# Thirteen sections of a fused Fourier and attention kernel: the same slots of the two row halves in another order

## The chip, the cores and the metric

The kernel runs on one core of a Trainium2 chip. The metric is the device time of one execution in microseconds (us): 1698.75 us, the median of 1699.33, 1698.75 and 1698.6.

## The reference, cut to what matters

The input is one sequence of 2048 tokens with 512 features. Two branches are mixed by a gate per token.

```python
g = _sigmoid((x * gate_w).sum(-1, keepdims=True))
a = _A_ref(x, ...)   # y = dft_seq_re @ (x @ dft_hid_re.T) - dft_seq_im @ (x @ dft_hid_im.T)
b = _B_ref(x, B_wqkv, B_wo)
return g * a + (1 - g) * b
...
H = 32; Dh = D // H                                  # 32 heads of 16 features
scores = jnp.einsum("bhqd,bhkd->bhqk", q, k) * scale
p = _softmax(scores, axis=-1)
o = jnp.einsum("bhqk,bhkd->bhqd", p, v)
return (lambda x, *d: x.transpose(*d))(o, 0, 2, 1, 3).reshape(B, S, D) @ wo
```

The last line's `@ wo` is the projection whose matmuls are the nine products of this document.

## The kernel before, in words

The kernel takes the heads in 16 pairs; one head of a pair lives in rows 0 to 63 of the matmul array, the other in rows 64 to 127. A matmul that contracts over only 64 rows occupies one half of the array, and two of them, one in each half, run side by side. All work of the main part is written as such pairs, in an order written out by hand; no scheduler changes it. Each engine executes its own list of instructions in that order.

There are four kinds of matmul in this part, each into one PSUM bank of 128x512.

- `a` (line 284, `a_tile`): keys by queries transposed the other way, to find the row maximum of the scores. VectorE reads the bank with a maximum reduction (line 286).
- `s` (line 774, `scores`): the scores with the maximum already subtracted through two extra rows. ScalarE reads the bank with the exponential into `pt` (line 775).
- the product (line 451, `Chain.mm`, tile `d`): in the sections that matter here a 64-row half of one of the nine products of a token tile's projection. Three head groups with three products each (high and low parts of the operands) make nine; each is done once in each half of the rows, so that eighteen matmuls add up in one bank of its own (`psD`, one buffer). After the eighteenth, `finish` (line 646) lets ScalarE scale the bank into `few`, and GpSimd adds it to the output tile (line 647).
- the values step (line 796, `pv`), written `|`: four heads' worth of `pt` times the values into one accumulating bank `acc`. Each fp32 matmul of it is recorded twice, so a step shows as eight.

`a` and `s` have three banks each, `psA` and `psS`. A new tile of a kind takes the bank of that kind that was used longest ago, so the fourth `a` waits until VectorE has read the first, and the fourth `s` until ScalarE has read the first.

A pattern is a text of slots, walked by `segment` (line 907) once for each row half; its first text is half 0, the second half 1. A slot of one letter is a pair: first a product in the current half, then a score (`s` or `a`) in the other half. A slot of two letters is a double: two scores and no product, the first letter in the other half and the capital in the current half. `|` is a values step. In half 1, the first product of a section waits for the reader of the scores that stood after the last product of half 0 (line 940), because the two halves of a sum may not be written into the bank at once. The product is issued before the score of its slot, and `finish` is issued right behind the eighteenth product, ahead of that slot's score.

Patterns follow each other: `START`, 13 times `THIN`, 96 times `FULL` (the Fourier sums over the sequence), 13 times `NINE`, and then a tail written out in `whole` (line 992). `NINE` takes nine products per section, eight sections from the projection of the second half of the tokens and five from the first. When the last maximum of a pair of heads and half of the tokens is issued, two follow-ups are put into `deferred`: `m_parts` (line 293: a small reduction on VectorE and two small operations on GpSimd) and `m_rows` (line 301: a transpose on VectorE and eight small DMAs that write the two extra rows of `qs`, on SP's queue and on GpSimd's). In a `NINE` section one of them is run behind the first `|` of a half that has a second one (line 925), or at the end of a half (line 949).

Of the kernel before, what the change touches and what calls it, by code (L numbers as in the profile page):

```python
# [31 lines left out]
def mix_kernel(ctx: ExitStack, tc: tile.TileContext, xa_t, xa, wqkv, w_hid, w_seq, wo, gate_w, out):  # L32
# [776 lines left out]
    def take(gen, n, whole=True):  # L809

        got = []
        while len(got) < n:
            x = next(gen, None)
            if x is None:
                break
            x[0].left -= 1
            got.append((*x, x[0].left == 0))
            if whole and got[-1][4]:
                break
        return got  # L820
# [56 lines left out]
    FULL = "s2 a3 s4 a1 s5 s2 a0 s3 a4 s1 a5 s2 a0 s3 a4 a1 | |"  # L877
    START = "sA s aS - - a s - - a s - - a", "s a s a s a s a s a s a +s +a"
    THIN = "s a s a s a s a s a | s a aS sA |", "aS a s s a s a s a s | s a a sA |"
    NINE = "a s a s a s a s a | sS sA aA |", "aS s a s a s s a aS | s a sA sA |"  # L880

    def stream(h):

# [23 lines left out]
    def segment(pattern, half, ds, stop):  # L907
# [5 lines left out]
        for n, slot in enumerate(pattern.split()):  # L913
# [3 lines left out]
            if slot == "|":  # L917
# [5 lines left out]
                while between:  # L923
                    between.pop(0)()
                if deferred and pattern in NINE and not turned and "|" in pattern.split()[n + 1:]:
                    deferred.pop(0)()
# [21 lines left out]

        if deferred and not (pattern in NINE and (turned or len(deferred) == 1)):
            deferred.pop(0)()  # L950

    def pairs():
# [5 lines left out]
        for gen, n in ((proj(1, (0, 1, 2), one), 8), (first, 5)):  # L958
            for i in range(n):
                yield NINE, take(gen, 9)  # L960

# [86 lines left out]
```

## Time and profile before

| what | value |
|---|---|
| runs | 1699.33, 1698.75, 1698.6 us |
| span of the profiled execution | 1696.8 us (its own device time is not listed; the runs lie 1.8 to 2.5 us above this span) |
| TensorE busy | 1689.2 us, 100% of the span |
| VectorE busy | 1366.7 us, 81% |
| ScalarE busy | 1138.6 us, 67% |
| GpSimd busy | 449.6 us, 26% |
| the 13 sections | 1489.68 to 1632.47 us of the span |
| the tail behind them | 1632.47 to 1696.80 us |

Times are counted from the start of the span. A matmul of 64 rows is recorded with 0.39 us, but two halves and two successive matmuls overlap, so busy time says little about TensorE: the distance between the starts of successive matmuls is what counts. A row of a timeline gives the start, the duration, the engine, the line, the operation, the tiles and, in brackets, the idle time of the engine before it with what ended that. PE is the matmul, PEld the load of its weights, DVE is VectorE, ACT is ScalarE, POOL is GpSimd, SP the queue that issues most DMAs.

### The profile page before, as it was taken

How to read it: one execution, taken by the hardware profiler on the slowest of the kernel's cores; microseconds unless marked ns; L12 is line 12 of the kernel's file. 1: busy time of each engine (PE TensorE's matmuls, PEld its weight loads, DVE VectorE, ACT ScalarE, POOL GpSimd, SP SyncE). 2: the span in 40 equal slices, each digit the busy share in tenths (PEclk: the TensorE clock that was granted, in tenths of full speed). 3: DMA queues.
4: the chain of work that ended last, by engine and by line, in shares of the span. 5: the costliest groups of instructions: out<-in, count | busy, mean ns of one | idle time of the engine just before them, and what ended most of it. 6: DMA issues, size and time to landing. Idle time of an engine off the chain costs nothing.

```text
span 1696.8 us, 33721 instructions
## 1 busy us (share of the span) xinstructions
PE 1689.2 (100%) x13040; PEld 1076.1 (63%) x13040; DVE 1366.7 (81%) x2313; ACT 1138.6 (67%) x2242; POOL 449.6 (26%) x554
## 2 busy tenths in 40 slices
PE   9999999999999999999999999999999999999998
PEld 7888855556666666666666666666666666655544
DVE  5439888888888888888888888888888888889854
ACT  5212377777766777666777677776667776678886
POOL 0101122322222333222222343322323343211110
PEclk9999999999999999999999999999999999999999
DMA  8963600314141434314156435224141535362114
GB/s 294 344 146 132 161 8 13 47 39 76 57 76 46 88 98 97 73 39 82 38 95 243 96 108 109 68 63 77 50 83 58 120 111 101 129 187 39 36 30 138
DMA packets 82274, 165.10 MB, mean 97 GB/s; under 512 B 19460, under 2 KB 19954, under 8 KB 78274
## 3 DMA queue, kind: packets, MB, share of 16 engines
q1 hardware_dynamic: 77874, 161.99, 37.1%
q8 instruction: 103, 1.69, 0.4%
q0 software_dynamic: 3808, 0.30, 0.2%
q10 hardware_dynamic: 432, 0.66, 0.1%
q14 instruction: 57, 0.47, 0.1%
HBM read 107.73 MB, written 54.52 MB: 96 GB/s over the span
## 4 chain that ended last, share of the span: by engine, by line
PE 99%; DMA 0%; DVE 0%; DVEq 0%; ACT 0%; SPq 0%; issue 0%
PE d L451 33%; PE acc L796 27%; PE s L774 14%; PE a L284 12%; PE s L365 3%; PE s L397 1%; PE d L365 1%; PE acc L782 1%; PE a L106 1%; PE s L107 1%; PE a L107 1%; PE s L106 1%; PE s L105 1%; PE a L105 1%; PE s L451 1%; PE a L451 0%
## 5 line engine op out<-in xcount | busy, mean ns | idle before, releaser
L286 DVE TENSOR_REDUCE mx<-a 128x1 f32<-128x512 f32 x2026 | 1239.9, 681 | 213.1 <-PE a L284 199.1
L775 ACT ACTIVATE pt<-s 128x512 f32<-128x512 f32 x2006 | 1023.2, 620 | 403.0 <-PE s L774 390.5
L774 PE MATMUL s<-qs,ks 50*128 50x512 f32 x2006 | 794.0, 422 | 0.0
L284 PE MATMUL a<-ks,qs 48*128 48x512 f32 x2026 | 744.5, 398 | 0.0
L451 PE MATMUL d<-xab,ch 64*128 64x512 f32 x2016 | 647.8, 396 | 0.0
L774 PEld LDWEIGHTS s<-qs,ks 50*128 50x128 f32 x2006 | 365.4, 185 | 228.5 <-issue 177.5
L796 PE MATMUL acc<-pt,vt 128*17 128x512 f32 x3968 | 484.2, 596 | 0.0
L284 PEld LDWEIGHTS a<-ks,qs 48*128 48x128 f32 x2026 | 370.3, 186 | 53.2 <-DVE mx L286 23.2
L451 PE MATMUL d<-xab,cl 64*128 64x512 f32 x1008 | 399.4, 396 | 0.0
L451 PEld LDWEIGHTS d<-xab,ch 64*128 64x128 f32 x2016 | 366.7, 184 | 21.6
L435 POOL CAST ch<-craw 128x512 fp32r<-128x512 f32 x126 | 77.1, 612 | 549.1 <-PE a L284 282.2
L796 PEld LDWEIGHTS acc<-pt,vt 128*17 128x17 f32 x3968 | 102.3, 96 | 184.7 <-issue 184.5
L451 PEld LDWEIGHTS d<-xab,cl 64*128 64x128 f32 x1008 | 185.7, 184 | 10.5
L436 POOL TENSOR_TENSOR cl<-craw,ch 128x512 fp32r<-128x512 f32 x126 | 162.1, 1287 | 10.2
L309 POOL DMA_DIRECT2D qs<-mt x119 | 67.0, 568 | 150.3 <-DVE mt L303 147.8
L451 PE MATMUL d<-wre,xab 64*128 64x512 f32 x336 | 90.5, 402 | 0.0
L451 PEld LDWEIGHTS d<-wre,xab 64*128 64x128 f32 x336 | 59.0, 185 | 38.4 <-issue 23.3
L451 PE MATMUL d<-wo_hl,o_hl 64*128 64x512 f32 (+1 forms) x246 | 68.1, 409 | 0.0
L451 PEld LDWEIGHTS d<-wo_hl,o_hl 64*128 64x128 f32 (+1 forms) x246 | 42.3, 185 | 29.5 <-issue 12.1
L101 ACT CAST hl<-s 128x512 fp32r<-128x512 f32 x28 | 16.1, 587 | 58.5 <-PE s L365 31.4
L647 POOL TENSOR_TENSOR yp<-yp,few 128x512 f32<-128x512 f32 x12 | 15.4, 1283 | 112.4 <-ACT few L646 112.4
L469 POOL CAST xab<-y 128x512 fp32r<-128x512 f32 x16 | 9.8, 611 | 127.8 <-ACT y L467 99.6
(168 smaller groups left out, 1009.6 us busy)
## 6 DMA issues: line engine op xcount, KB each, us to landing
craw<-w_seq SPq DMA_DIRECT2D x128, 256.0 KB
qk<-hl SPq DMA_DIRECT2D x32, 512.0 KB
qs<-qk SPq DMA_DIRECT2D x96, 128.0 KB
ks<-qk SPq DMA_DIRECT2D x96, 128.0 KB
b<-hl SPq DMA_DIRECT2D x16, 512.0 KB
xab<-b SPq DMA_DIRECT2D x16, 512.0 KB
o<-oe SPq DMA_DIRECT2D x62, 128.0 KB
oh<-nh SPq DMA_DIRECT2D x12, 512.0 KB
```

The costliest lines, as they stand in the source:

```text
L105: nc.tensor.matmul(ps, sh, mh, start=first, stop=False)
L106: nc.tensor.matmul(ps, sh, ml, start=False, stop=False)
L284: nc.tensor.matmul(ps, qs[p % 2][r, qt * P:(qt + 1) * P], ks[p % 2][r, kb * 512:(kb + 1) * 512], start=True, stop=True)
L286: user = nc.vector.tensor_reduce(mx[p % 2][:, h, qt, kb:kb + 1], ps, AX.X, ALU.max)
L309: (nc.gpsimd if own else nc.sync).dma_start(rows.rearrange("v (q b c) -> v b q c", q=8, b=4)[:, b], mt[hf][32 * b + h:32 * b + 32:2])
L365: i = nc.tensor.matmul(ps, st[r], mv[r], start=not half and not j, stop=half == 1 and j == 11)
L435: nc.gpsimd.tensor_copy(h1, raw)
L436: nc.gpsimd.tensor_tensor(l1, raw, h1.bitcast(F32), ALU.subtract)
L451: i = nc.tensor.matmul(self.ps, st[r], mv[r], start=not self.begun, stop=stop)
L774: nc.tensor.matmul(ps, ks[p % 2][rr, kt * P:(kt + 1) * P], qs[p % 2][rr, q0:q0 + 512], start=True, stop=True)
L775: return nc.scalar.activation(pts[u][:, 2 * qb + h], ps, AF.Exp, bias=0.0, scale=DH ** -0.5)
L796: i = nc.tensor.matmul(acc[32 * j:32 * j + 17], vt[:, kt, p, 16 * h:16 * h + 17], pt[:, j], start=kt == 0, stop=kt == NT - 1)
```

## The change

Only the text of the pattern `NINE` changes. A section keeps 18 single slots and 7 doubles, 16 `s`, 16 `a` and four values steps, and each stream of scores keeps its count in each section. What changes is the order, and so where the doubles stand and how many `a` stand near each other.

```diff
     FULL = "s2 a3 s4 a1 s5 s2 a0 s3 a4 s1 a5 s2 a0 s3 a4 a1 | |"
     START = "sA s aS - - a s - - a s - - a", "s a s a s a s a s a s a +s +a"
     THIN = "s a s a s a s a s a | s a aS sA |", "aS a s s a s a s a s | s a a sA |"
-    NINE = "a s a s a s a s a | sS sA aA |", "aS s a s a s s a aS | s a sA sA |"
+    NINE = "s a s a s s a aS | aS a s sA |", "aS aA sS | sA a s s a a a s a s |"
```

Before, half 0 is nine singles, a values step, three doubles and a values step; half 1 is a double, seven singles and a double, a values step, two singles and two doubles, and a values step. After, half 0 is seven singles and a double, a values step, a double, two singles and a double, and a values step; half 1 is three doubles, a values step, a double and nine singles, and a values step. The lists of GpSimd and SP are the same in both kernels; those of TensorE, ScalarE and VectorE differ only in the order within the sections, and at the last section's end.

## The prediction

> **What bounds the kernel now.** I read the page first, for the engine that carries the span.
>
> ```profile
> span 1696.8 us, 33721 instructions
> PE 1689.2 (100%) x13040; PEld 1076.1 (63%) x13040; DVE 1366.7 (81%) x2313; ACT 1138.6 (67%) x2242; POOL 449.6 (26%) x554
> PE 99%; DMA 0%; DVE 0%; DVEq 0%; ACT 0%; SPq 0%; issue 0%
> ```
>
> TensorE makes 99% of the chain that ended last. So what counts is where its list stands still. Next the view by windows, for four sections (busy time and count per engine, then the granted clock), and the row of `few`, the reader of each section's sum:
>
> ```profile
> 1500.63:1511.71 11.08, 11.08 (x86) 5.54 (x82) 10.07 (x19) 8.82 (x19) 3.86 (x8) 1.00 0.21 78
> 1511.71:1522.74 11.03, 11.03 (x87) 5.59 (x83) 9.91 (x17) 9.23 (x20) 1.30 (x2) 1.00 0.42 71
> 1533.66:1544.58 10.92, 10.92 (x88) 5.55 (x84) 9.84 (x17) 8.84 (x19) 1.28 (x2) 1.00 0.18 61
> 1621.55:1632.47 10.92, 10.92 (x82) 5.26 (x79) 7.84 (x13) 8.83 (x19) 3.07 (x4) 1.00 0.24 69
> L646 ACT ACTIVATE few<-d,omg x13: 681/682/682, 1499.6 to 1631.4; 128x512 f32<-128x512 f32 x13
> ```
>
> Twelve distances in 131.8 us: a section takes 10.98 us. VectorE is busy for 9.8 to 10.1 of that (third group), so it has one microsecond to spare, on average over the section only.
>
> The timeline of one section gives the prices of TensorE:
>
> ```profile
> 1534.00 0.39 PE L774 MATMUL s<-qs,ks 50*128 50x512 f32 x1
> 1535.40 0.40 PE L774 MATMUL s<-qs,ks 50*128 50x512 f32 x1
> 1535.64 0.42 PE L284 MATMUL a<-ks,qs 48*128 48x512 f32 x1
> 1536.97 0.72 PE L774 MATMUL s<-qs,ks 50*128 50x512 f32 x3
> 1538.85 0.50 PE L284 MATMUL a<-ks,qs 48*128 48x512 f32 x1
> 1539.20 0.50 PE L774 MATMUL s<-qs,ks 50*128 50x512 f32 x1
> 1540.23 0.40 PE L774 MATMUL s<-qs,ks 50*128 50x512 f32 x1
> 1540.56 0.50 PE L774 MATMUL s<-qs,ks 50*128 50x512 f32 x1
> 1540.90 0.39 PE L284 MATMUL a<-ks,qs 48*128 48x512 f32 x1
> 1542.46 0.50 PE L774 MATMUL s<-qs,ks 50*128 50x512 f32 x1
> 1543.26 0.39 PE L284 MATMUL a<-ks,qs 48*128 48x512 f32 x1
> 1544.58 0.50 PE L284 MATMUL a<-ks,qs 48*128 48x512 f32 x1
> ```
>
> Pair to pair: six in 1.40 us (1534.00 to 1535.40), 0.235 each. Across a values step: 1535.64 to 1536.97 and 1543.26 to 1544.58, 1.32. The pair behind a step needs 0.34 to the next, since its weights are not loaded ahead: it is recorded with 0.50 in place of 0.39, so it truly runs 0.11 later than recorded. Any pair that waits pays the same 0.11 again (1540.56 with 0.50, next at 1540.90).
>
> **The change part by part.** A section has 25 pairs in four stretches, before and after. Without waits it takes 4 x (0.34 + 1.32) + (25 - 8) x 0.235 = 10.64 us in either order. So the old order holds 0.34 us of waits, and the question is what the new order holds.
>
> The waits are for banks. Their clocks are the readers':
>
> ```profile
> 1537.77 4.87 DVE L286 TENSOR_REDUCE mx<-a 128x1 f32<-128x512 f32 x8 [0.47 <-PE a L284]
> 1501.36 0.68 DVE L286 TENSOR_REDUCE mx<-a 128x1 f32<-128x512 f32 x1
> 1501.96 0.68 DVE L286 TENSOR_REDUCE mx<-a 128x1 f32<-128x512 f32 x1
> 1502.10 0.18 PEld L284 LDWEIGHTS a<-ks,qs 48*128 48x128 f32 x1
> 1502.69 0.18 PEld L284 LDWEIGHTS a<-ks,qs 48*128 48x128 f32 x1 [0.16 <-DVE mx L286]
> 1489.68 0.50 PE L284 MATMUL a<-ks,qs 48*128 48x512 f32 x1
> 1490.25 3.08 DVE L286 TENSOR_REDUCE mx<-a 128x1 f32<-128x512 f32 x5 [0.82 <-PE a L284]
> 1490.03 0.39 PE L774 MATMUL s<-qs,ks 50*128 50x512 f32 x1
> 1490.45 2.06 ACT L775 ACTIVATE pt<-s 128x512 f32<-128x512 f32 x4 [1.54 <-PE s L774]
> ```
>
> A reduction lasts 0.68 and the next starts (4.87 - 0.68) / 7 = 0.60 later. The fourth and fifth `a` load their weights 0.05 to 0.06 after the ends, 2.04 and 2.64, of the reductions three before them. So an `a` is recorded no earlier than the start of the third reduction before it plus 0.73, and truly runs 0.11 later. The first `a` behind a values step meets its reduction after 0.57; a later one after 0.46. An `s` meets its exponential after 0.42; exponentials follow every (2.06 - 0.60) / 3 = 0.49.
>
> *Removed.* The four-`s` run in old half 1 (wait 1540.23 to 1540.56, and its 0.11: 0.2 together) and the wait of the first product in half 1 (1538.85 to 1539.20 is behind a step, and 1539.20 again carries 0.50: 0.11). That is 0.31 of the 0.34. In the new order that product stands behind eight more scores, so its condition is long met.
>
> *Added, the run of `a`.* Number the new section's slots 1 to 25. After the third values step come 16 `sA`, 17 `a`, 18 `s`, 19 `s`, 20 `a`, 21 `a`, 22 `a`, 23 `s`, 24 `a`, 25 `s`. Count from slot 16. Without waits: slots 17 to 25 at 0.34, 0.58, 0.81, 1.05, 1.28, 1.52, 1.75, 1.99, 2.22, next section at 3.54. Reductions: of 16 at 0.57, of 17 at 1.17, of 20 at 1.77. Slot 21 needs the bank of 16: 0.57 + 0.73 = 1.30, truly 1.41, 0.13 late. Slot 22 needs that of 17: 1.90, truly 2.01 in place of 1.64: another 0.37. Then 23 at 2.25, 24 due at 2.48 needs 20's: 2.50, truly 2.61: 0.13. So 25 stands at 2.85, the next section at 4.17: **+0.63**.
>
> *Added, three doubles in a row.* From slot 9 (first behind a step): reductions of 9, 10 and 12 at 0.57, 1.17, 1.77. Slot 13 comes at 0.81 + 1.32 = 2.13, slot 14 at 2.47; its second `a` needs the bank of 12: 2.50, truly 2.61: **+0.14**. The `s` waits of half 0 (slots 6 and 8) come to 0.02 each, **+0.04**.
>
> Sum: 10.64 + 0.63 + 0.14 + 0.04 = 11.45 us a section, against 10.98: **+0.46**. The same arithmetic on the old order gives 10.96 to 11.06, so I trust it to about 0.05.
>
> *Moved, the end of the sum.* The eighteenth product now stands in the last slot, and the next section's first product needs its bank back from `few`. Before, two singles' rest and two doubles lay between.
>
> ```profile
> 1499.07 0.60 ACT L775 ACTIVATE pt<-s 128x512 f32<-128x512 f32 x1 [0.56 <-PE s L774]
> 1499.56 0.68 ACT L646 ACTIVATE few<-d,omg 128x512 f32<-128x512 f32 x1
> 1542.46 0.18 PEld L451 LDWEIGHTS d<-wo_hl,o_hl 64*128 64x128 f32 x1 [0.85 <-issue]
> 1544.57 0.18 PEld L451 LDWEIGHTS d<-wo_hl,o_hl 64*128 64x128 f32 x1 [0.85 <-ACT few L646]
> ```
>
> The 0.85 before 1544.57 is put down to `few`, but 1542.46 has the same 0.85 with no `few`: it is the values step. In the new order, product 25 truly runs at 2.85; taking the 0.42 of an exponential, `few` starts at 3.28, ends at 3.96, frees the bank at 4.01; the product is due at 4.17. Hidden by the values step, with 0.16 to spare. If `few` were half a microsecond later, about 0.35 would show; both ends are kept.
>
> *Moved, the follow-ups and their DMAs.* The lists of GpSimd and SP do not change. The transpose comes behind four reductions of half 0 in place of five.
>
> ```profile
> 1504.58 2.73 SPq L309 DMA_DIRECT2D qs<-mt  x4
> 1504.85 2.24 POOL L309 DMA_DIRECT2D qs<-mt  x4 [2.81 <-DVE mt L303]
> 1515.03 0.50 PE L774 MATMUL s<-qs,ks 50*128 50x512 f32 x2
> qs<-mt POOLq DMA_DIRECT2D x119, 2.0 KB, 1.7
> ```
>
> The rows are written from 1504.58 on and first used at 1515.03, a section later; the issues end by 1507.3, a landing takes 1.7. New first use: slot 8, 1.75 us into its section, where it was at 3.3 (1511.71 to 1515.03). Some 5 us of cover remain; price nothing.
>
> *Last section.* One half's `a` stream runs out: the section in the row 1621.55 has 12 reductions. In the new order slots 20 to 24 lose their `a`, so its run costs nothing: 10.82 against 10.92, -0.1. The tail keeps its list; its start meets one exponential less in ScalarE's queue and an earlier last maximum; 0, within 0.3.
>
> Total: 12 x 0.46 - 0.1 = **+5.4 us**. The span goes from 1696.8 to 1702.2; the median of the runs lies 1.95 above the span, which I keep: 1704.1 us.
>
> *A rule against the change.* All quoted windows show the clock at 1.00, with waits in them. The Trainium skill, "TensorE: Matmul & The Clock Gate", section "A second HAM failure mode: psum-queue depth-cycling", says that cycling through PSUM banks can let TensorE idle briefly so often that its clock drops back to half. No run here shows it. If it held, a pair would cost 0.47: 25 x 0.235 x 13 = 76 us more, by estimate some 1780 us.
>
> **The rivals.** *The waits are dearer:* `few` shows as well, 0.35 more in each of twelve sections: 5.4 + 4.2 = +9.6, 1708.4 us. Against it stand the 0.16 to spare.
>
> *The waits are half as dear:* a waiting `a` does not pay the 0.11, because the product ahead of it in its slot is already running. Then the run costs 0.37, the doubles nothing: 10.64 + 0.41 = 11.05 to 11.18, at most +0.2 a section, +2.3: 1701.0 us. For it: slot 22's product is issued before its wait. Against it: 1540.56, where exactly that happened.
>
> *Faster:* the banks of the `a` run come free in time, in slots 21 to 24. Then only the removed waits count: 10.82 or less against 10.98, -0.16 x 13 = -2 to, without any wait, -4.4: 1694.3 us. It decides when the new waits, 0.81 by my sum, stay under 0.34 a section. With reductions 0.45 apart in place of 0.60 the run alone would still hold 0.35, and the row of eight shows 0.60.
>
> *The clock rule* above is the last.
>
> **How the numbers follow.** Forecast, +0.3 to +0.6 a section, 0.68; dearer 0.10; half as dear 0.14; faster 0.07; clock 0.01. The likeliest gives 1704.1. The range runs from the half-price end, 1701.0, to just under the dear end, 1708.0. A measurement tells about 0.2%, 3.4 us: the first two and the clock are slower, 0.79; half price falls within, 0.14; faster 0.07.
>
> **What would show it.** The distance of `few` rises to 11.4; weight loads of `a` wait on the reduction in slots 21, 22 and 24, with 0.3 to 0.4 in slot 22; the waits of line 451 on the exponential in half 1 vanish; the 0.85 before a section's first product stays 0.85 (a higher number is the dear rival); the clock stays 1.00. I am wrong if reductions start sooner after their `a` than 0.46, or if waits are hidden behind the products.

## The result and the profile after

The changed kernel takes 1703.36 us, the median of 8 runs (1702.99 to 1703.73), against 1698.66 us for the kernel before on the same chip: a ratio of 1.0027, with a 95% interval of 1.0017 to 1.0038. The forecast was 1704.1 us, slower, with a range of 1701.0 to 1708.0.

The page of the changed kernel, its span and its busy times per engine:

```profile
span 1701.5 us, 33708 instructions
PE 1693.1 (100%) x13040; PEld 1068.7 (63%) x13040; DVE 1368.5 (80%) x2313; ACT 1140.5 (67%) x2242; POOL 449.6 (26%) x554
```

The span is 4.7 us longer. The counts of instructions per engine are those of before, and the busy times of VectorE and ScalarE are 1.8 and 1.9 us higher: hardly anything was added but waiting. The view by windows puts it in its place. First the kernel before, then the changed one; each has the thirteen sections in the first row and the tail in the second (busy time and count per engine, the granted clock, the DMAs):

```profile
1489.68:1632.47 142.79, 142.79 (x1066) 71.85 (x1063) 126.74 (x211) 115.40 (x224) 25.98 (x35) 1.00 0.28 75
1632.47:1696.80 64.33, 58.17 (x381) 27.37 (x377) 24.88 (x44) 46.57 (x95) 7.40 (x6) 0.99 0.30 97
```

```profile
1489.87:1637.17 147.30, 146.88 (x1067) 69.03 (x1063) 128.08 (x212) 117.55 (x224) 25.73 (x35) 1.00 0.27 72
1637.17:1701.50 64.33, 58.15 (x381) 27.32 (x377) 24.50 (x42) 46.39 (x94) 7.66 (x6) 0.97 0.32 98
```

The sections grow by 4.51 us, the tail is the same to the hundredth, and 0.19 lies ahead of the first section. The clock stays at 1.00 in the sections; in the tail it is 0.97 in place of 0.99, with the same length.

The timeline of one section of the changed kernel: its first product, the first pair behind each values step, then the waiting `a` of the last stretch, the section's eighteenth product beside the last of them, and the next section's first product:

```profile
1535.35 0.49 PE L451 MATMUL d<-wo_hl,o_hl 64*128 64x512 f32 x1
1538.43 0.49 PE L284 MATMUL a<-ks,qs 48*128 48x512 f32 x1
1540.56 0.50 PE L284 MATMUL a<-ks,qs 48*128 48x512 f32 x1
1542.54 0.50 PE L774 MATMUL s<-qs,ks 50*128 50x512 f32 x1
1543.85 0.50 PE L284 MATMUL a<-ks,qs 48*128 48x512 f32 x1
1544.45 0.50 PE L284 MATMUL a<-ks,qs 48*128 48x512 f32 x1
1545.05 0.49 PE L284 MATMUL a<-ks,qs 48*128 48x512 f32 x1
1545.05 0.49 PE L451 MATMUL d<-wo_hl,o_hl 64*128 64x512 f32 x1
1546.69 0.50 PE L451 MATMUL d<-wo_hl,o_hl 64*128 64x512 f32 x1
```

The section takes 11.34 us. Its stretches take 3.08, 2.13, 1.98 and 4.15; the prediction's terms for them add up to 3.11, 2.13, 2.04 and 4.17. Counted from slot 16 (1542.54), slots 21, 22 and 24 stand at 1.31, 1.91 and 2.51; the prediction had 1.30, 1.90 and 2.50. The three stand 0.60 apart, which is the distance of VectorE's reductions and none of the 0.235, 0.34 and 1.32 of TensorE's pairs.

The weight loads of that stretch say the same, and the end of a section shows `few`:

```profile
1544.45 0.18 PEld L284 LDWEIGHTS a<-ks,qs 48*128 48x128 f32 x1 [0.41 <-DVE mx L286]
1545.05 0.18 PEld L284 LDWEIGHTS a<-ks,qs 48*128 48x128 f32 x1 [0.30 <-DVE mx L286]
1546.69 0.18 PEld L451 LDWEIGHTS d<-wo_hl,o_hl 64*128 64x128 f32 x1 [0.85 <-ACT few L646]
...
1545.72 0.68 ACT L646 ACTIVATE few<-d,omg 128x512 f32<-128x512 f32 x1
```

`few` ends at 1546.40, 0.29 before the first product of the next section, whose 0.85 is the usual idle time behind a values step.

Last, the waits of TensorE's weight loads over all sections (engine, tile and line, what it waited for: us in total, times, longest). Before:

```profile
PEld a L284 <- DVE mx L286: 11.5, 16, 0.9
PEld d L451 <- ACT pt L775: 1.2, 8, 0.2
PEld s L774 <- ACT pt L775: 1.2, 5, 0.3
```

and after:

```profile
PEld a L284 <- DVE mx L286: 30.9, 51, 0.9
PEld s L774 <- ACT pt L775: 11.0, 13, 0.9
```

These lists also hold the 0.85 of idle time behind a values step, put down to whatever came last. Of the 16 waits of `a` before, 13 are such 0.85, and of the 51 after, 26. Without them the waits of `a` for VectorE rise from 3 of 0.16 us to 25 of 0.24 to 0.41: from 0.5 to 8.8 us. The 13 waits of `s` after are 0.85 too, so the 5 of before, up to 0.3, are gone, and those of a product for an exponential, which the prediction expected to go, are in the list no more.

### The profile page after: what moved, and what is told of

Read it like the earlier page. It is cut to its first block, busy times and chain, and to the rows that moved or that the text cites. A ratio compares the mean times of both kernels' runs of the same rounds, so it can differ in the third digit from the quotient of the medians.

```text
span 1701.5 us, 33708 instructions
## 1 busy us (share of the span) xinstructions
PE 1693.1 (100%) x13040; PEld 1068.7 (63%) x13040; DVE 1368.5 (80%) x2313; ACT 1140.5 (67%) x2242; POOL 449.6 (26%) x554
## 4 chain that ended last, share of the span: by engine, by line
PE 99%; DMA 0%; DVE 0%; issue 0%; DVEq 0%; ACT 0%; SPq 0%
PE d L451 33%; PE acc L796 27%; PE s L774 14%; PE a L284 13%; PE s L365 3%; PE s L397 1%; PE d L365 1%; PE acc L782 1%; PE s L106 1%; PE s L105 1%; PE a L106 1%; PE a L105 1%; PE a L107 1%; PE s L107 1%; PE s L451 1%; PE a L451 0%
```

## The experiments

The theory: a bank comes free at the pace of its reader, 0.60 us for VectorE's reduction, and an `a` that comes before the third reduction ahead of it has ended waits for that. The rivals are named in each expectation. All experiments compare with the same kernel before, at 1698.6 to 1698.75 us. The section's length is taken from the first and the last of the thirteen `few`, divided by twelve.

### The five `a` of the last stretch set apart

```diff
-    NINE = "s a s a s s a aS | aS a s sA |", "aS aA sS | sA a s s a a a s a s |"
+    NINE = "s a s a s s a aS | aS a s sA |", "aS aA sS | sA a s a s a s a s a |"
```

> The nine singles of half 1 in the changed kernel become a s a s a s a s a: the five a stand apart, and the last of them stands in the last slot. Theory (VectorE's pace of 0.60 us sets when a bank comes free): counted from slot 16, slots 21, 23 and 25 each come 0.13 late (banks of 16, 17 and 19 at 1.30, 1.90, 2.50), slot 25 at 2.61 in place of 2.85. The section falls by 0.24, from the 11.34 measured to 11.10; about 2.9 us less than the changed kernel, some 1700.5. Rival (TensorE itself is slow where a follows a in the same half): all of the run's cost goes, section 10.8, about 1697.

Measured: 1700.39 us, ratio 1.001 (1.000 to 1.0019). The row of `few` and three weight loads of one section:

```profile
L646 ACT ACTIVATE few<-d,omg x13: 680/682/712, 1500.3 to 1634.0; 128x512 f32<-128x512 f32 x13
...
1543.57 0.18 PEld L284 LDWEIGHTS a<-ks,qs 48*128 48x128 f32 x1 [0.22 <-DVE mx L286]
1544.17 0.18 PEld L284 LDWEIGHTS a<-ks,qs 48*128 48x128 f32 x1 [0.30 <-DVE mx L286]
1545.58 0.18 PEld L451 LDWEIGHTS d<-wo_hl,o_hl 64*128 64x128 f32 x1 [0.85 <-ACT few L646]
```

The section takes 133.7 / 12 = 11.14 us. Set apart, the `a` still wait, 0.60 from each other; what is gained is only that the last of them stands in the last slot, with the values step behind it. That is the theory's number, and not the rival's 10.8.

### The run split, its last `a` where it was

```diff
-    NINE = "s a s a s s a aS | aS a s sA |", "aS aA sS | sA a s s a a a s a s |"
+    NINE = "s a s a s s a aS | aS a s sA |", "aS aA sS | sA a s s a a s a a s |"
```

> Only the slots 22 and 23 of the changed kernel change places: a s s a a s a a s. The three neighbouring a are split, the number of a ahead of the last one is the same. Theory (VectorE's pace): banks come free at the same times; slot 21 is 0.13 late, slot 23 0.13, slot 24 0.36, together 0.62 as before: section 11.34, time equal to the changed kernel within 0.5 us, some 1703.4. Rival (neighbouring a are dear on TensorE): the run is broken, so the section loses 0.2 to 0.4, 2.4 to 5 us less than the changed kernel.

Measured: 1703.13 us, ratio 1.0027 (1.0017 to 1.0037).

```profile
L646 ACT ACTIVATE few<-d,omg x13: 687/687/687, 1500.1 to 1636.3; 128x512 f32<-128x512 f32 x13
...
1544.38 0.18 PEld L284 LDWEIGHTS a<-ks,qs 48*128 48x128 f32 x1 [0.22 <-DVE mx L286]
1544.98 0.18 PEld L284 LDWEIGHTS a<-ks,qs 48*128 48x128 f32 x1 [0.41 <-DVE mx L286]
```

The section takes 11.35 us, as in the changed kernel. The wait has only moved from one `a` to the next (0.22 and 0.41 here, 0.41 and 0.30 there). Neighbouring `a` cost TensorE nothing by themselves.

### Shorter reads by VectorE, in both orders

The same edit in the changed kernel and in the kernel before; `short` is true in the thirteen sections:

```diff
-        user = nc.vector.tensor_reduce(mx[p % 2][:, h, qt, kb:kb + 1], ps, AX.X, ALU.max)
+        user = nc.vector.tensor_reduce(mx[p % 2][:, h, qt, kb:kb + 1], ps[:, :256] if short else ps, AX.X, ALU.max)
```

> The changed kernel, but in the thirteen sections VectorE's maximum reads only 256 of a bank's 512 columns (the maximum of the other half is left out). From a reduction of 64 elements at 0.22 us and one of 512 at 0.68 I estimate 0.41 us each, one every 0.33. Theory: the waits for banks of a go, only about 0.1 is left; section 10.7 to 10.8, some 7 us less than the changed kernel and 2 to 3 us less than the kernel before: 1696. Rival (the order costs on TensorE, or through few): the section stays at 11.3, 1703.

> The kernel before with the same half reads (the maximum of 256 columns is left out in the thirteen sections). Theory: its waits are for the exponential, not for VectorE; the section falls by 0.03 to 0.1 only, 0.4 to 1.3 us, to 1697.4 to 1698.3. If its waits were for VectorE too, it would fall by about 0.3 a section, 4 us. Beside the changed kernel with half reads it should be the slower of the two by about 2 us.

Measured: 1695.13 us for the new order, ratio 0.998 (0.9971 to 0.999), and 1697.76 us for the old, ratio 0.9996 (0.9986 to 1.0005). The groups of the reduction and the rows of `few`, in the new order and then in the old:

```profile
L287 DVE TENSOR_REDUCE mx<-a 128x1 f32<-128x256 f32 x194 | 73.4, 420 | 56.1 <-PE a L285 38.6 <-PE s L775 14.4 <-PE d L452 2.6
L647 ACT ACTIVATE few<-d,omg x13: 680/683/688, 1499.8 to 1628.5; 128x512 f32<-128x512 f32 x13
```

```profile
L287 DVE TENSOR_REDUCE mx<-a 128x1 f32<-128x256 f32 x191 | 75.6, 422 | 53.4 <-PE a L285 45.1 <-PE d L452 5.6 <-PE s L775 0.5
L647 ACT ACTIVATE few<-d,omg x13: 680/681/682, 1499.5 to 1630.6; 128x512 f32<-128x512 f32 x13
```

A reduction of 0.42 us in place of 0.68 takes 0.62 from a section of the new order (11.34 to 10.72) and 0.06 from one of the old (10.98 to 10.92). So the whole loss hangs on VectorE's reduction. And with shorter reductions the new order is the faster one, by 2.6 us: the waits that it removes were real, as the prediction's "faster" rival had it, but the condition of that rival is not met at 0.60.

### The three doubles mixed, alone and with the singles set apart

```diff
-    NINE = "s a s a s s a aS | aS a s sA |", "aS aA sS | sA a s s a a a s a s |"
+    NINE = "s a s a s s a aS | aS a s sA |", "aS sA aS | sA a s s a a a s a s |"   # alone
+    NINE = "s a s a s s a aS | aS a s sA |", "aS sA aS | sA a s a s a s a s a |"   # both
```

> Only the three doubles of the changed kernel become aS sA aS, so that no double holds two a. Theory (VectorE's pace): the second a of slot 14 no longer comes too early for its bank; the profile of the changed kernel shows 0.08 lost there (1.98 from slot 13 to slot 16, 1.90 without waits), my sum had 0.14. The section falls from 11.34 to 11.20 to 11.26, 1 to 1.7 us, some 1702. Rival (three doubles in a row are slow on TensorE whatever they hold): the section stays at 11.34.

> Both: doubles aS sA aS and singles a s a s a s a s a. Theory: the gains add, 11.34 - 0.24 - 0.08 = 11.02 a section, within 0.05 of the order before (10.98); some 1699.4. Rival (one gain makes the other void, since the run then starts with VectorE further behind): 11.10, as with the singles alone, 1700.4.

Measured: 1701.71 us, ratio 1.0018 (1.0009 to 1.0028), for the doubles alone; 1699.14 us, ratio 1.0002 (0.9992 to 1.0011), for both.

```profile
L646 ACT ACTIVATE few<-d,omg x13: 681/681/682, 1499.6 to 1634.5; 128x512 f32<-128x512 f32 x13
```

```profile
L646 ACT ACTIVATE few<-d,omg x13: 681/682/713, 1500.0 to 1632.4; 128x512 f32<-128x512 f32 x13
```

The sections take 11.24 and 11.03 us. The double `aA` costs 0.1, the run 0.2 more than the spread order, and the two add. With both undone, seven products still stand first, three doubles still stand in a row and the sum still ends in the last slot, and the kernel is as fast as before within what can be measured. That tie is a balance, not the absence of waits: the spread `a` still wait three times 0.13, which with the 10.64 of a section without waits makes the 11.03, and the old order had 0.34 of other waits. That the moved products and doubles themselves cost next to nothing is shown by the half reads, whose 10.72 lies 0.08 above 10.64. What costs is where the `a` stand among them.

### `few` done twice

```diff
-            nc.scalar.activation(tmp, ps, AF.Copy, scale=omg[:, t:t + 1])
+            for _ in range(2 if maxima_left else 1):
+                nc.scalar.activation(tmp, ps, AF.Copy, scale=omg[:, t:t + 1])
```

> The changed kernel with the operation on few done twice, so that the sum's bank comes free 0.57 us later. Theory (few is hidden, 0.26 to spare in the profile of the changed kernel: few from 1534.36 to 1535.04, first product at 1535.35): 0.57 - 0.26 = 0.31 shows in each of twelve sections, which rise to 11.65; +3.7 us, some 1707. Rival (few is already what the first product waits for, as the profile's label of its 0.85 says): all 0.57 shows, +6.8 us, 1710.

Measured: 1709.22 us, ratio 1.0062 (1.0047 to 1.0077): 5.9 us above the changed kernel, where the theory had 3.7 and the rival 6.8. By these numbers alone the rival is the nearer one, so the rows have to decide:

```profile
1547.54 1.40 ACT L647 ACTIVATE few<-d,omg 128x512 f32<-128x512 f32 x2
1548.99 0.18 PEld L451 LDWEIGHTS d<-wo_hl,o_hl 64*128 64x128 f32 x1 [1.33 <-ACT few L647]
```

The expectation's price of the doubling was wrong. I had taken the 0.57 after which an exponential follows `few`; a second `few` into the same tile starts 0.72 later (1.40 for the two, 0.68 for one). Of these 0.72 the idle time shows 1.33 - 0.85 = 0.48, in twelve sections 5.8 us. So 0.24 was hidden, which agrees with the 0.24 to 0.29 to spare in the changed kernel (0.29 from the end of `few` to the first product, less the 0.05 from a reader's end to the next weight load). The rival, by which nothing is hidden, would have shown all 0.72, 8.6 us. This working with 0.72 was done after the run.

### A larger dose

```diff
-    NINE = "s a s a s s a aS | aS a s sA |", "aS aA sS | sA a s s a a a s a s |"
+    NINE = "s a s a s s a aS | aS a s sA |", "aS aA sS | sA s s s s a a a a a |"
```

> A larger dose: the nine singles of half 1 become s s s s a a a a a, so the s run four in a row and the a five. Theory (a bank comes free at its reader's pace, 0.60 for a and 0.49 for s): by the same sum as in the prediction the s wait 0.74 and the last two a 0.97 in all, and the section rises by 1.08 over the changed one, to 12.4; +13 us, some 1716. Rival (only VectorE and the number of a in the stretch count, not where they stand): 11.34, 1703.

Measured: 1716.36 us, ratio 1.0104 (1.0088 to 1.0121).

```profile
L646 ACT ACTIVATE few<-d,omg x13: 687/687/689, 1501.0 to 1649.3; 128x512 f32<-128x512 f32 x13
...
1546.84 0.18 PEld L774 LDWEIGHTS s<-qs,ks 50*128 50x128 f32 x1 [0.85 <-ACT pt L775]
1548.03 0.18 PEld L774 LDWEIGHTS s<-qs,ks 50*128 50x128 f32 x1 [0.43 <-ACT pt L775]
1548.52 0.18 PEld L774 LDWEIGHTS s<-qs,ks 50*128 50x128 f32 x1 [0.30 <-ACT pt L775]
1550.04 0.18 PEld L284 LDWEIGHTS a<-ks,qs 48*128 48x128 f32 x1 [0.75 <-DVE mx L286]
1550.63 0.18 PEld L284 LDWEIGHTS a<-ks,qs 48*128 48x128 f32 x1 [0.41 <-DVE mx L286]
1552.04 0.18 PEld L451 LDWEIGHTS d<-wo_hl,o_hl 64*128 64x128 f32 x1 [0.85 <-ACT few L646]
```

The section takes 12.36 us against the 12.4 expected. The `s` wait at ScalarE's 0.49 from one to the next, the last `a` at VectorE's 0.59 (1548.03 to 1548.52, 1550.04 to 1550.63). The numbers of `a` and of `s` in the stretch are unchanged, so the places of the two alone make 1 us a section; this order makes the `s` wait as well, so it doesn't price the `a` by themselves.

With full reads none of these orders is faster than the kernel before; the best one ties with it.

## Why the prediction was right

The direction, the size and the place were right: +4.7 us against a forecast of +5.4.

- *What is removed.* The old order's 0.34 us of waits a section were taken to be ScalarE's, 0.31 of them in two places. The half reads in the old order, which moved its section by 0.06 only, show that most of them are not VectorE's, and the waits of products and of `s` for an exponential are gone from the changed kernel's list. No run made ScalarE itself faster.
- *The run of `a`*, forecast +0.63 in its stretch. Slots 21, 22 and 24 came within 0.01 us of the times written down, and the stretch within 0.02. Shown by the profile, by the half reads, by splitting and spreading the run, and by the larger dose.
- *Three doubles in a row*, forecast +0.14. The stretch was 1.98 where 1.90 needs no wait: +0.08. Undoing it gave back 0.1 and left a stretch of 1.88. The term was too large by 0.04 to 0.06.
- *The `s` waits of half 0*, forecast +0.04: the stretch of 3.08 is 0.03 shorter than the sum; they did not show.
- *The base.* With these small terms the section shown takes 11.34, 0.11 less than the sum's 11.45. The forecast set that sum for one plain section against the old mean of 10.98, though a plain old section, the one of its timeline, takes 10.92. Plain against plain the sum says +0.53 and the traces +0.42. The means grew by 0.40: twelve sections take 1626.50 - 1489.87 = 136.63 us, 11.39 each, against 10.99 before by the same count. So the mean hid 0.06 of the 0.11, and to that extent it is luck that the total came within 0.7 us.
- *`few` hidden by the values step*, forecast 0.16 to spare: 0.24 to 0.29 by the profile and by the doubling. The prediction let the eighteenth product run with its slot, at 2.85. But a product is issued ahead of the score of its slot, and here it ran beside the waiting `a` of slot 24, at 2.51, so that `few` started at 3.18 and not at 3.28. The dear rival falls with it.
- *The follow-ups and their DMAs* at nothing: the tail, which has the last of them, is 64.33 us in both kernels, and no weight load of the sections waits for a DMA.
- *The last section*, forecast -0.1: it takes 1626.50 to 1637.17, 10.67 in place of 10.92, so -0.25. Half of the missing 0.15 is the terms that are too large in every section (0.03 and 0.05), the other 0.07 the last stretch, 3.47 where the sum has 3.54:

```profile
1633.70 0.49 PE L774 MATMUL s<-qs,ks 50*128 50x512 f32 x1
1637.17 0.91 PE L774 MATMUL s<-qs,ks 50*128 50x512 f32 x3
```

- *Ahead of the sections* 0.19 us were not in the forecast. The work ahead of them is the same in every kernel here, and in the ten traces their first product stands between 1489.37 and 1490.00: 0.19 is within what one execution differs from the next.
- *A side sum.* By the prediction's own arithmetic reductions 0.45 apart would leave the run 0.60 and not 0.35, because the reduction of slot 20 can't start before 1.28 + 0.46 = 1.74, and slot 24 needs that bank: another 0.25. It speaks against the "faster" rival only the more.

The sum of what was measured: 12 x 0.397 - 0.25 + 0.19 = 4.7 us. The rival by which a waiting `a` pays no 0.11 for its weights had +2.3 us and is out: rows with 0.50 stand at each wait. The clock rule of the Trainium skill ("TensorE: Matmul & The Clock Gate", section "A second HAM failure mode: psum-queue depth-cycling") did not come into play: with 25 waits of `a` for VectorE of up to 0.41 us in the sections, besides the 0.85 behind each values step, the granted clock of the sections stayed 1.00.

## What to carry to other kernels

When two engines pass work through a few banks, an order costs something where the producer asks for a bank before the reader, at its own pace, has come to the end of it. Write these times down slot by slot; here the stretches came out within 0.06 us. And set the sum for a plain section against a plain section, not against a mean. An average with room to spare (VectorE was busy for 9.9 of 11 us) says nothing about a stretch in which the reader's work stands close together. And a bank's release that lies behind other work can be moved up to the end of that work for nothing, here 0.24 us from showing.

## What the runs showed of the hardware that I had not expected

Two ScalarE operations from the same bank into the same tile `few` started 0.72 us apart, where operations on different banks and tiles started 0.49 to 0.57 apart. Whether the shared tile, the shared bank or the operation is the reason, no run here shows. The working of the doubling above rests on the 0.72.

Work of VectorE that the old order hid seems to show in the new one. A reciprocal of 0.54 us stands among the reductions of the twelfth section, here in the changed kernel's timeline with that section's two `few`:

```profile
1614.01 0.68 ACT L646 ACTIVATE few<-d,omg 128x512 f32<-128x512 f32 x1
1625.53 0.68 ACT L646 ACTIVATE few<-d,omg 128x512 f32<-128x512 f32 x1
1622.53 0.54 DVE L568 RECIPROCAL rc<-rc 128x64 f32<-128x64 f32 x1
```

They are 11.52 apart, where most are 11.34 to 11.43. In the kernel before, the two around the same operation were 10.94 apart, as most. With half reads, in the new order, the reciprocal (1614.78) stands ahead of the last stretch's reductions too, and the section is not longer: its two `few`, at 1607.10 and 1617.79, are 10.69 apart, the others 10.71 to 10.74. That fits a reciprocal that costs something only where VectorE's pace already holds TensorE up. That it is the cause is argued from this and from its place, behind which the run of `a` begins; no experiment removed the reciprocal itself.
